# One transfer instead of seven for three chunks of w_down, in a decode step of attention and GEGLU FFN

## The chip, the cores and the metric

The kernel runs on one core of a Trainium2 chip. The metric is the device time of one execution in microseconds, as a median of runs. Beside it stands the profile of one execution, with the span from its first to its last instruction.

## The reference, cut to what matters

Two sequences (B = 2) each have one new token of D = 640 features. 32 heads of 192 attend to the last 2,048 of 8,192 cached positions; then follows a GEGLU FFN of width F = 1,536. All tensors are bfloat16.

```python
W = min(4096, max(256, Sk // 4))            # 2048 of Sk = 8192
q = (ln(x) @ wq).reshape(B, 1, 32, 192).transpose(0, 2, 1, 3)
k, v = k_cache[:, :, Sk - W:], v_cache[:, :, Sk - W:]
p = softmax(einsum("bhqd,bhkd->bhqk", q, k) * 192 ** -0.5)
o = einsum("bhqk,bhkd->bhqd", p, v)
h = x + o.transpose(0, 2, 1, 3).reshape(B, 1, 6144) @ wo
out = h + (gelu(ln(h) @ w_gate) * (ln(h) @ w_up)) @ w_down
```

Here `ln` is a layernorm without weights. Nearly all bytes are K and V, 50 MB each inside the window; the weights come to 21.6 MB.

## The kernel before, in words

**Memory.** All large inputs pass through one ring in SBUF, `ring` (L174): 128 partitions of 122,880 bytes. `load` (L251) gives each load the next place in the ring and puts it in a list. `pump` (L258) takes loads from this list in order and records one DMA for each on SP's queue (L272), as soon as the readers of the place's old content have been recorded; the DMA then waits on the chip until those readers are done. `done` (L275) marks a load as read and calls `pump`. So all transfers run in one order, on one queue: K of 16 groups of heads and V of the same groups alternating (3 MB each), with Wq near the start and Wo in between, and at the end Wo, w_gate, w_up and w_down. A group is four heads of one sequence.

**Parts.** A load may be cut along the partitions: `parts` is a list of ranges of partitions, and L271 to L273 issue one DMA for each range, with a completion semaphore of its own from a set of 32. A matmul that reads such a load waits for all of its parts. Only w_down uses this: `load_ffn` (L302) loads w_down (F x D, 1.97 MB) in four chunks of three of the twelve row blocks (`WDC`, L147), 480 KB each, with 3,840 bytes in each partition. For chunks 0 to 2 (`WDB = 3`, L149) the list `WDP` (L150) applies: partitions 0 to 111 in one DMA, then five DMAs of three partitions, then one of a single partition. Chunk 3 goes as one DMA of 128 partitions. In all these are 22 DMAs.

**Compute.** For each group, `transposes` turns K on TensorE through PSUM, ScalarE and VectorE copy it to SBUF, `scores`, `softmax` and `e_columns` give the weights, and `pv` (L571) multiplies V. After every four groups `o_rows` and `o_columns` arrange the result, and `oproj` (L616) multiplies it with Wo. `wo_parts` (L299) says in how many parts Wo of eight heads is loaded and multiplied: one of 12 rows per partition, or, for the last eight heads, two of 8 and 4.

**The end.** After the last `oproj`, `h_columns` (L643) and a layernorm give the FFN's input. `ffn_in` (L691) multiplies it with w_gate (20 matmuls, L697), `ffn_columns` (L703) turns the result by a copy on VectorE (L704) and three transposes (L708), and `h_rows` (L714) puts the residual into PSUM. A chain of small steps on VectorE and ScalarE then computes gelu of the gate. The second `ffn_in` takes w_up, `ffn_columns` again, and a product gives `uT`. Last, L737 to L747 multiply `uT` with w_down chunk by chunk, 12 matmuls each (L743), add to the residual in PSUM, and a copy (L749) and two small stores (L751) write the output. The order of the work on each engine is that in which the program records it.

Of the kernel before, what the change touches and what calls it, by code (L numbers as in the profile page):

```python
# [13 lines left out]
D = 640  # L14
# [28 lines left out]
class _Prog:  # L43
# [10 lines left out]

    def op(self, eng, fn, R=(), W=(), X=(), dma=None):
        o = _Op(eng, fn)
        deps = []

        def add(y, same_ok):
            if y is None or y is o:  # L60
                return
            if y.dma_sem is None and y.eng == eng and dma is None and same_ok:
                return
            deps.append(y)

        for t in R:
            add(self.w.get(t), eng == "pe")
        for t in W:
            add(self.w.get(t), eng == "pe")
            for y in self.r.get(t, ()):  # L70
                add(y, True)
        for t in X:
            for e, y in self.x.get(t, {}).items():
                if e != eng:
                    add(y, True)
        for t in R:
            self.r.setdefault(t, []).append(o)
        for t in W:
            self.w[t] = o
            self.r[t] = []  # L80
        for t in X:
            self.x.setdefault(t, {})[eng] = o
        if dma is not None:
            o.dma_sem = dma
            self.dma_count[dma] = self.dma_count.get(dma, 0) + 16
            o.dma_val = self.dma_count[dma]
        o.deps = deps
        lst = self.per.setdefault(eng, [])
        o.idx = len(lst) + 1
        lst.append(o)  # L90
        self.ops.append(o)
        return o
# [51 lines left out]
NSEM = 32  # L144
# [1 line left out]
WQC = ((0, 2), (2, 4), (4, 5))  # L146
WDC = ((0, 3), (3, 6), (6, 9), (9, 12))  # L147
BIG = 1.0e9
WDB = 3  # L149
WDP = ((0, 112), (112, 115), (115, 118), (118, 121), (121, 124), (124, 127), (127, 128))  # L150


def bass_sequential_preLN__sliding_block_cached__geglu_ffn__decode_kernel(
# [12 lines left out]
    with ExitStack() as ctx:  # L166
# [78 lines left out]
        P = _Prog()  # L245


        pos = [0, 0]
        where, live, queue, used = {}, [], [], set()

        def load(key, nbytes, src, shape, parts=((0, 128),)):  # L251
            if pos[0] + nbytes > RING:
                pos[0] = 0
            off, i = pos[0], pos[1]
            pos[0], pos[1] = off + nbytes, i + len(parts)
            queue.append((key, off, nbytes, src, shape, i, parts))

        def pump():  # L258
            while queue:
                key, off, nbytes, src, shape, i, parts = queue[0]  # L260
                old = [q for q in live if q[1] < off + nbytes and off < q[1] + q[2]]
                if any(q[0] not in used for q in old):
                    return
                for q in old:
                    live.remove(q)
                queue.pop(0)
                live.append((key, off, nbytes))
                v = shape(ring[:, off // 2:(off + nbytes) // 2])
                toks = [("ring", x) for x in range(off // GRAN, (off + nbytes + GRAN - 1) // GRAN)]
                where[key] = (v, toks + [("part", key, n) for n in range(1, len(parts))])  # L270
                for n, (p0, p1) in enumerate(parts):  # L271
                    P.op("sp", lambda e, v=v[p0:p1], src=src[p0:p1] if n or len(parts) > 1 else src: e.dma_start(v, src),  # L272
                         W=(toks if n == 0 else [("part", key, n)]) + [("sem", (i + n) % NSEM)], dma=f"d{(i + n) % NSEM}")  # L273

        def done(*keys):  # L275
            used.update(keys)
            pump()
# [5 lines left out]
        def load_k(g):  # L283
            load(("k", g), 2 * TPG * DH, kv_src(A_k_cache, g), lambda v: v)

        def load_v(g):
            load(("v", g), 2 * TPG * DH, kv_src(A_v_cache, g), lambda v: v)

        def load_wq():
            wq = A_wq.rearrange("(p c) n -> p c n", c=NC5)  # L290
            for i, (c0, c1) in enumerate(WQC):
                load(("wq", i), 2 * (c1 - c0) * HQ * DH, wq[:, c0:c1, :], lambda v: v.rearrange("p (c n) -> p c n", n=HQ * DH))
# [9 lines left out]
        def load_ffn():  # L302
            for key, w in (("wg", B_w_gate), ("wu", B_w_up)):
                load(key, 2 * NC5 * F, w.rearrange("(p c) f -> p c f", c=NC5),
                     lambda v: v.rearrange("p (c f) -> p c f", c=NC5))
            wd = B_w_down.rearrange("(r p j) n -> r p j n", p=128, j=3)
            for i, (f0, f1) in enumerate(WDC):
                load(("wd", i), 2 * (f1 - f0) * D, wd[i],
                     lambda v: v.rearrange("p (s n) -> p s n", n=D), WDP if i < WDB else ((0, 128),))


        def dve(fn, R=(), W=(), X=()):
            return P.op("dve", fn, R, W, X)

        def act(fn, R=(), W=(), X=()):
            return P.op("act", fn, R, W, X)
# [26 lines left out]
        load_wo(2)  # L343
        load_wo(3)
        load_ffn()
        pump()

        BITS = (1, 2, 3, 6, 12, 16, 28, 31, 32, 64, 96)
# [463 lines left out]
```

## Time and profile before

| What | Value |
|---|---|
| Median of 3 runs | 299.38 us (299.14 to 299.56) |
| Profiled execution, its own time | 299.38 us |
| Span of the profiled execution | 297.5 us |
| Mean granted TensorE clock | 0.83 |
| Busy: PE, PEld, DVE, ACT, POOL | 66%, 51%, 44%, 32%, 1% of the span |
| DMA, whole span | 122.61 MB, mean 412 GB/s |
| K and V transfers | 16 each, 3,072 KB; issue to landing 31.6 and 28.3 us (medians) |
| w_gate and w_up | 1,920 KB each; issue to landing 32.8 and 27.6 us |
| w_down issues | 3 of 420 KB, 1 of 480 KB, 15 of 11.2 KB, 3 of 3.8 KB |

PE is TensorE's matmuls and PEld its weight loads; DVE is VectorE, ACT ScalarE, POOL GpSimd, and SPq the queue of SyncE, which issues the DMAs. A line number stands for a line of the kernel. The 16 DMA engines of the core are given as one mean share. The trace also has a record of each DMA packet (start, duration, bytes; here one row of one partition), without its engine, and of each time that a DMA engine reports its part of a transfer done, which is called a landing record below.

### The profile page before, as it was taken

Reading aid. Unit: us, or ns where it says so; the run is one execution under the profiler, and the core shown is the slowest. Engines: PE = TensorE matmul, PEld = TensorE weight load, DVE = VectorE, ACT = ScalarE, POOL = GpSimd, SP = SyncE. Lnnn points to the kernel's source line nnn. Section 1 sums busy time; section 2 is a strip of 40 time slices with the busy share of each in tenths; the row PEclk is TensorE's granted clock in tenths of the full one; section 3 lists DMA queues with packets and bytes.
Section 4 is the critical chain, followed back from the end, with each engine's and each line's share of the span. In section 5 each row is a group of like instructions: output and inputs, shape, how many; then the busy total and the mean of one; then the engine's idle time right before and its main releaser. Section 6 shows DMA issues by size and latency. Waiting matters only on the chain.

```text
span 297.5 us, 4923 instructions
## 1 busy us (share of the span) xinstructions
PE 197.7 (66%) x2141; PEld 152.1 (51%) x2141; DVE 130.6 (44%) x326; ACT 95.5 (32%) x119; POOL 2.7 (1%) x19
## 2 busy tenths in 40 slices
PE   2473668749497497759591888774878674957554
PEld 1451266719294475456560858471748471934311
DVE  5950455716247154425263353461473461533121
ACT  2150134715233163325251324452324361420000
POOL 3000000000000000000000000000000000000000
PEclk9997559998869599959796695999797998697655
DMA  7999999999999999999999999999999999999993
GB/s 285 443 434 419 423 426 438 430 432 433 419 422 433 443 426 423 433 416 433 435 433 430 419 436 422 433 428 433 430 425 433 432 430 422 430 426 413 425 232 111
DMA packets 6713, 122.61 MB, mean 412 GB/s; under 512 B 802, under 2 KB 804, under 8 KB 1444
## 3 DMA queue, kind: packets, MB, share of 16 engines
q1 hardware_dynamic: 6680, 122.29, 97.7%
q8 instruction: 17, 0.28, 0.4%
q14 instruction: 4, 0.03, 0.0%
q10 hardware_dynamic: 12, 0.00, 0.0%
HBM read 122.29 MB, written 0.00 MB: 411 GB/s over the span
## 4 chain that ended last, share of the span: by engine, by line
DMA 69%; PE 20%; SPq 5%; DVE 3%; issue 1%; ACT 0%
DMA ring<-in_A_k_cache_dram 53%; PE tps L479 17%; DMA ring<-in_A_wq_dram 9%; DMA ring<-in_B_w_down_dram 6%; SPq L272 5%; PE ops L577 1%; DVE rq L331 1%; DVE ktr L491 1%; PE tps L501 1%; DVE ering L331 0%; PE m L628 0%; PE m L610 0%; PE ops L519 0%; ACT qrow L508 0%; PE m L591 0%
## 5 line engine op out<-in xcount | busy, mean ns | idle before, releaser
L479 PE MATMUL tps<-identf,ring 128*128 128x128 f32 x768 | 116.2, 320 | 45.9 <-DMA ring<-in_A_k_cache_dram 45.0
L479 PEld LDWEIGHTS tps<-identf,ring 128*128 128x128 f32 x768 | 107.5, 169 | 49.2 <-DMA ring<-in_A_k_cache_dram 46.2
L488 ACT ACTIVATE ktr<-tps 128x1024 bf16<-128x1024 bf16 x80 | 79.2, 1023 | 87.1 <-PE tps L479 86.6
L491 DVE COPY ktr<-tps 128x1024 bf16<-128x1024 bf16 x112 | 74.4, 688 | 73.8 <-PE tps L479 73.1
L552 ACT ACTIVATE eexp<-sm,nm 128x512 bf16<-128x512 f32 x16 | 11.5, 721 | 66.8 <-DVE nm L550 66.8
L577 PE MATMUL ops<-ring,ering 128*32 128x384 bf16 x512 | 24.9, 338 | 5.6 <-DMA ring<-in_A_v_cache_dram 5.5
L541 DVE CUSTOM_DVE_ANT_1 sm<-sps,mska 128x512 f32<-128x512 f32 x16 | 11.1, 691 | 36.2 <-PE sps L535 36.2
L535 PE MATMUL sps<-ktr,rq 128*16 128x512 bf16 x384 | 26.0, 405 | 0.3 <-DVE rq L331 0.3
L577 PEld LDWEIGHTS ops<-ring,ering 128*32 128x32 bf16 x512 | 12.7, 99 | 14.2 <-DMA ring<-in_A_v_cache_dram 6.8
L535 PEld LDWEIGHTS sps<-ktr,rq 128*16 128x16 bf16 x384 | 9.5, 90 | 11.5 <-issue 2.8
L548 PEld LDWEIGHTS m<-mrhs,pm 128*128 128x128 bf16 x16 | 1.5, 96 | 25.0 <-DVE mrhs L327 25.0
L548 PE MATMUL m<-mrhs,pm 128*128 128x16 bf16 x16 | 2.9, 184 | 16.9 <-DVE mrhs L327 16.9
L501 PE MATMUL tps<-ring,xnT 128*32 128x384 bf16 x80 | 5.7, 444 | 7.3 <-DMA ring<-in_A_wq_dram 7.3
L331 DVE TENSOR_TENSOR rq<-ops,mask 128x96 bf16<-128x96 f32 x16 | 2.7, 248 | 14.3 <-PE ops L519 14.3
L331 DVE TENSOR_TENSOR ering<-m,mask 128x256 bf16<-128x256 f32 x16 | 6.7, 420 | 2.4 <-PE m L561 2.4
L501 PEld LDWEIGHTS tps<-ring,xnT 128*32 128x32 bf16 x80 | 2.3, 119 | 10.2 <-DMA ring<-in_A_wq_dram 8.4
L383 ACT ACTIVATE lt<-m,eps_t 128x2 f32<-128x2 f32 x2 | 0.5, 262 | 19.4 <-PE m L381 19.4
L561 PE MATMUL m<-sel,eexp 128*128 128x64 bf16 x64 | 4.8, 201 | 1.2 <-ACT eexp L552 1.2
L628 PE MATMUL m<-ring,ot 128*2 128x320 bf16 x96 | 4.1, 298 | 1.9 <-DMA ring<-in_A_wo_dram 1.9
L331 DVE TENSOR_TENSOR orow<-m,wm 128x1536 bf16<-128x1536 f32 x3 | 5.3, 1751 | 0.0
L561 PEld LDWEIGHTS m<-sel,eexp 128*128 128x128 bf16 x64 | 4.4, 105 | 1.6 <-DVE nm L550 1.3
L610 PE MATMUL m<-selb,orow 128*128 128x2 bf16 x48 | 3.5, 200 | 2.2 <-DVE ering L331 1.6
(112 smaller groups left out, 79.6 us busy)
## 6 DMA issues: line engine op xcount, KB each, us to landing
ring<-in_A_k_cache_dram SPq DMA_DIRECT2D x16, 3072.0 KB, 31.6
ring<-in_A_v_cache_dram SPq DMA_DIRECT2D x16, 3072.0 KB, 28.3
ring<-in_A_wq_dram SPq DMA_DIRECT2D x2, 3072.0 KB, 20.9
ring<-in_A_wo_dram SPq DMA_DIRECT2D x3, 1920.0 KB, 27.7
ring<-in_B_w_gate_dram SPq DMA_DIRECT2D x1, 1920.0 KB, 32.8
ring<-in_B_w_up_dram SPq DMA_DIRECT2D x1, 1920.0 KB, 27.6
ring<-in_A_wq_dram SPq DMA_DIRECT2D x1, 1536.0 KB, 27.8
ring<-in_A_wo_dram SPq DMA_DIRECT2D x1, 1280.0 KB, 28.0
```

What stands on the lines that cost most here:

```text
L272: P.op("sp", lambda e, v=v[p0:p1], src=src[p0:p1] if n or len(parts) > 1 else src: e.dma_start(v, src), W=(toks if n == 0 else [("part", k ...
L331: return lambda e: e.tensor_tensor(out=out, in0=a, in1=b, op=op)
L479: ins = e.transpose(tps[bi][:, 128 * u:128 * (u + 1)], kv[:, off:off + 128], identf[:, :])
L488: act(lambda e, dst=dst, bv=bv: e.activation(out=dst, in_=bv, func=ACT.Copy), W=[("kt", slot, n)], X=[("t", bi)])
L491: dve(lambda e, dst=dst, bv=bv: e.tensor_copy(dst, bv), W=[("kt", slot, n)], X=[("t", bi)])
L501: ins = e.matmul(tps[0][32 * r:32 * (r + 1), 0:384], lhsT=xnT[:, c, 32 * J:32 * (J + 1)], rhs=wq[:, c - c0, 1536 * J + 384 * r:1536 * J + ...
L535: ins = e.matmul(sps[32 * ch:32 * ch + 16, :], lhsT=rq[:, g, k, :], rhs=ktr[:, g % 2, k // 2, 1024 * ch + k % 2:1024 * (ch + 1):2], start= ...
L541: dve(lambda e: e.tensor_tensor_reduce(out=sm[:, :].rearrange("p (u x) -> p u x", u=4), in0=sps[:, :].rearrange("p (u x) -> p u x", u=4), ...
L548: pe(lambda e: e.matmul(m2[:, 256:272], lhsT=pm[:, :], rhs=mrhs[:, :], start=True, stop=True), R=["pm", "mrhs"], X=["m2"])
L552: act(lambda e: e.activation(out=eexp[:, :], in_=sm[:, :], func=ACT.Exp, bias=nm[:, 0:1], scale=1.0, accum_out=zr[:, g // 4 % 2, g % 4:g % ...
L561: ins = e.matmul(o, lhsT=eexp[:, 128 * u:128 * (u + 1)], rhs=sel64[:, :], start=True, stop=True)
L577: ins = e.matmul(ops_[32 * r:32 * (r + 1), 0:384], lhsT=ering[:, g % 4, t, :], rhs=vv[:, 384 * t:384 * (t + 1)], start=(g % 4 == 0 and t < 4),
```

## The change

The list of parts is taken out of `load` and `pump`, and with it `WDB` and `WDP`. Each load is one DMA of 128 partitions and has one semaphore. So w_down is loaded with four DMAs of 480 KB instead of 22. The places in the ring, the order of the loads and the matmuls stay; only the numbers of the semaphores shift. Wo of the last eight heads is loaded and multiplied in two parts of 8 and 4 rows per partition in both kernels.

```diff
-WDB = 3
-WDP = ((0, 112), (112, 115), (115, 118), (118, 121), (121, 124), (124, 127), (127, 128))
...
-        def load(key, nbytes, src, shape, parts=((0, 128),)):
+        def load(key, nbytes, src, shape):
...
-            pos[0], pos[1] = off + nbytes, i + len(parts)
-            queue.append((key, off, nbytes, src, shape, i, parts))
+            pos[0], pos[1] = off + nbytes, i + 1
+            queue.append((key, off, nbytes, src, shape, i))
...
-                where[key] = (v, toks + [("part", key, n) for n in range(1, len(parts))])
-                for n, (p0, p1) in enumerate(parts):
-                    P.op("sp", lambda e, v=v[p0:p1], src=src[p0:p1] if n or len(parts) > 1 else src: e.dma_start(v, src),
-                         W=(toks if n == 0 else [("part", key, n)]) + [("sem", (i + n) % NSEM)], dma=f"d{(i + n) % NSEM}")
+                where[key] = (v, toks)
+                P.op("sp", lambda e, v=v, src=src: e.dma_start(v, src), W=toks + [("sem", i % NSEM)],
+                     dma=f"d{i % NSEM}")
...
-                     lambda v: v.rearrange("p (s n) -> p s n", n=D), WDP if i < WDB else ((0, 128),))
+                     lambda v: v.rearrange("p (s n) -> p s n", n=D))
```

More of the change, by code (lines that the diff above doesn't have):

```diff
@@ L254, in load @@
             off, i = pos[0], pos[1]
-            pos[0], pos[1] = off + nbytes, i + len(parts)
-            queue.append((key, off, nbytes, src, shape, i, parts))
+            pos[0], pos[1] = off + nbytes, i + 1
+            queue.append((key, off, nbytes, src, shape, i))
         def pump():
             while queue:
-                key, off, nbytes, src, shape, i, parts = queue[0]
+                key, off, nbytes, src, shape, i = queue[0]
                 old = [q for q in live if q[1] < off + nbytes and off < q[1] + q[2]]
```

## The prediction

> **What bounds the kernel now.** I first read the page's busy slices, then its chain of waits, then the end of the chain in order of time, then tables of short windows over the last 20 us. The page says that the DMA engines carry the run, and that something happens in its last two slices:
>
> ```profile
> DMA  7999999999999999999999999999999999999993
> GB/s 285 443 434 419 423 426 438 430 432 433 419 422 433 443 426 423 433 416 433 435 433 430 419 436 422 433 428 433 430 425 433 432 430 422 430 426 413 425 232 111
> ...
> DMA 69%; PE 20%; SPq 5%; DVE 3%; issue 1%; ACT 0%
> ```
>
> The reader should see that the last slice but one (282.6 to 290.1 us) is as busy as all others, at 9 tenths, but moves 232 GB/s instead of about 425. The engines are not idle there; they are slow. The chain ends on a w_down transfer, one group of matmuls and the output:
>
> ```profile
> 275.53 18.62 DMA ring<-in_B_w_down_dram
> 294.15 0.04 issue
> 294.19 0.60 PE m L743 x10
> ```
>
> The 5% of SPq ahead of this in the chain is the 22 w_down issues, one after another. It is not a cause. The last issue, at 275.53, joined a queue that had 11 us or more of earlier packets before it; its first packets ran near 288. The table by windows of 2 us (stretch, length, busy time of PE, PEld, DVE, ACT, POOL, then granted clock, DMA share, GB/s) shows when the loss begins:
>
> ```profile
> 280.00:282.00 2.00, 0.59 (x2) 0.50 (x2) 0.63 (x5) 0.47 (x2) 0.00 (x0) 0.50 0.99 415
> 282.00:284.00 2.00, 1.77 (x20) 0.52 (x20) 0.13 (x2) 0.00 (x0) 0.00 (x0) 0.50 1.03 311
> 284.00:286.00 2.00, 1.41 (x11) 0.57 (x11) 1.04 (x5) 0.00 (x0) 0.00 (x0) 0.50 1.02 238
> 286.00:288.00 2.00, 0.00 (x0) 0.00 (x0) 0.83 (x4) 0.22 (x1) 0.00 (x0) 0.50 1.00 230
> 288.00:290.00 2.00, 1.48 (x20) 0.51 (x20) 0.00 (x0) 0.00 (x0) 0.00 (x0) 0.50 0.97 204
> ```
>
> The packet records (start, duration, bytes) give the moment: the first packet of 3,840 bytes, a w_down row, starts at 282.27. Until then a w_up or w_gate row of 15,360 bytes takes 573 to 587 ns. From then on such rows, of the very same w_up transfer, take 629, 704, 855 and then 909 to 1,039 ns, on all nine engines that still work on w_up. w_down rows start at 149 ns and take 230 to 340 ns between 283 and 290.4. Those nine are behind: the landing records of w_gate show seven engines done at 278.16 to 279.11 and nine at 281.06 to 281.48; of w_up, seven at 282.77 to 284.09 and nine at 287.49 to 288.48.
>
> [...] 16 landings for a 112-row part, 3 for a 3-row part, 1 for the single row. [...] Inside the 112-row parts the durations swing between 149-160 ns and 200-250 ns in steps of a few rows, for all active engines together (291.4 fast, 291.75 slow, 292.0 medium, 292.3 slow), and from 292.8, when only the last chunk (128 partitions) is left, nearly all rows take 149 ns, with 12 engines at work. That chunk has the same row size and comes from the same tensor.
>
> **The change, part by part.** Wo: both kernels load and multiply Wo of the last heads in two parts of 8 and 4 rows; no line of that changes. Cost 0. What changes is w_down chunks 0 to 2: each goes from seven DMAs to one of 128 partitions.
>
> Issues on SP: 18 fewer, of 0.24 to 1.83 us each. The four that stay take some 0.4 us each after 261.28; the fourth waits for PE's work on group 14 (ends 262.29), so all are out near 263, not 276.6. Gain at the end 0: the queue is served in order and full until 282.27. If this cover were gone, no issue would start the data sooner than 282.27 either. Nothing else waits behind them on SP but the output store at 295.
>
> PE waits: 18 fewer semaphore checks. In the timeline 24 weight loads over two chunks took 0.63 us, 12 of the last chunk 0.23; the 14 waits of the first two cost at most 0.17 us, and they lie ahead of a wait for data. Value 0, bounds 0 and -0.2.
>
> w_down rows: [...] For the nine late engines that is 3 x 149 = 0.45 us more work at the undisturbed duration.
>
> The slowdown: here I choose full speed, as for every 128-partition transfer in this trace, the Wo parts (5,120-byte rows at 196 to 206 ns) among them. Bounds of this term: no slowdown left, or all of it left (the rivals).
>
> Sum for the nine late engines. w_gate lands at 281.48 on the last of them. w_up: 8 rows x 577 ns = 4.62 us, so 286.10 (check: the first engine went from 278.16 to 282.77, 4.61 us, mostly undisturbed). w_down: 4 chunks x (8 x 149 ns + some 20 ns for the completion) = 4 x 1.21 = 4.84 us, so the last chunk lands at 290.94, against 294.15 now.
>
> Does PE keep up? Now the second FFN product starts 0.04 after w_up lands, at 288.52:
>
> ```profile
> 288.52 1.77 PE L697 MATMUL ops<-ring,hnT 128*2 128x384 bf16 x20 [2.59 <-DMA ring<-in_B_w_up_dram]
> ...
> 292.06 1.63 PE L743 MATMUL m<-ring,uT 128*2 128x160 bf16 x36 [0.34 <-DVE uT L331]
> 294.19 0.57 PE L743 MATMUL m<-ring,uT 128*2 128x160 bf16 x12 [0.50 <-DMA ring<-in_B_w_down_dram]
> 294.81 0.33 DVE L749 CAST yrow<-m 98x160 bf16<-98x160 f32 x1 [2.81 <-PE m L743]
> ```
>
> With w_up at 286.10 it starts at 286.14 (h_rows before it ends at 285.93, so PE is free). The copy after it on DVE needs the gate's chain done: that ends at 287.18, before 287.95. From its start to the first down product is 292.06 - 288.52 = 3.54 us, so down starts at 289.68. Three chunks issue in about 0.63 + 0.26 = 0.9 us, to 290.6. The fourth is then the wait that ends last: 290.94 + 0.04 = 290.98 in place of 294.19. All after it is as now, so the gain is 3.21 us. The profiled execution took 299.38 with a span of 297.5; it equals the median of the runs. 299.38 - 3.21 = **296.2 us**, span 294.3.
>
> This has a floor: if w_down came at once, PE would start the fourth chunk at 290.6, 0.4 us earlier; if w_up did too, h_rows' end saves 0.17 more. Hence 295.6.
>
> **Rivals.**
> (a) Partly: slow in part for another reason, such as rows of only 3,840 bytes from a tensor being read beside w_up. At 200 ns a row instead of 149, 32 rows take 6.4 us: landing 286.10 + 6.4 = 292.5, gain 1.65, time 297.7. For it: the 112-row parts showed 174 to 220 ns in between. Against: Wo's 5,120-byte rows, beside other transfers, were undisturbed, and the last chunk ran at 149.
> (b) Slower: the slowdown comes from reading w_down at all, in whatever parts, while more than 12 engines are active. For it: the rate rose when four engines had finished near 290.4. Then w_up stays slow, and the late engines have three more rows of some 270 ns, 0.81 us, on the tail: 294.15 becomes 294.96, time 300.2. It decides from a mean row of about 201 ns if w_up stays slow too: from w_up's last packets near 287.2 to the end of the last row at 293.66 there is room for 32 rows of 201 ns. Against: 12 engines ran chunk 1 at 149 to 160 ns for a while (290.6 to 290.9), and with it, slower again, until 292.7; a limit by the number of engines would not swing.
> (c) No difference: half-way between (a) and (b), rows at about 230 ns with w_up undisturbed: 286.10 + 32 x 0.23 = 293.5, landing near 294; time 299.3.
>
> **How the numbers follow.** Forecast 68%, own range 295.5 to 297.0; its lower end is the floor, its upper end rows of some 175 ns, as in the better stretches of the 112-row parts (286.10 + 32 x 0.175 = 291.7, time 297.0); the runs shown spread over 0.42 us. (a) 13%, 297.0 to 298.8; (c) 5%, 298.8 to 300.0; (b) 14%, above 300.0. The range goes from the floor less a tenth, 295.5, to 298.9, the far end of (a), and leaves out some 2 in 10. A measurement of this kernel can tell about 0.2% (0.6 us) from no change: faster 81%, same 5%, slower 14%.
>
> **What would show it.** Right: in the windows from 282 to 286 the rate stays above 400 GB/s; no w_up row exceeds some 600 ns; w_up's wait ends near 286.1; w_down rows take about 150 ns, and the last lands near 291. Wrong: rows of 230 ns or more and 240 GB/s from 282.3 on, though every transfer has 128 partitions; then the split was a relief for the late engines, not the cause.

## The result, and the profile after

The changed kernel takes 296.08 us (median of 6 runs, 295.85 to 296.27), the kernel before 299.43 in the same comparison (299.06 to 299.62). The ratio is 0.9889, with a 95% interval from 0.9877 to 0.9902: 3.35 us less. The profiled execution has a span of 294.3 us, against 297.5. The forecast was 296.2, with a span of 294.3.

First the page's line of transfer rates in 40 slices, which answers to the one of before:

```profile
DMA  7999999999999999999999999999999999999992
GB/s 268 431 429 445 449 428 426 428 426 424 426 418 433 423 438 431 428 424 438 433 416 446 430 424 423 428 428 430 428 426 431 430 438 423 428 431 411 429 407 113
```

The slice that moved 232 GB/s at full business now moves 407. The table by windows of the changed kernel (stretch, length, busy time of PE, PEld, DVE, ACT, POOL, granted clock, DMA share, GB/s) has the same stretches as the one of before:

```profile
280.00:282.00 2.00, 0.78 (x3) 0.60 (x3) 0.66 (x4) 0.26 (x1) 0.00 (x0) 0.50 1.01 422
282.00:284.00 2.00, 1.51 (x20) 0.51 (x20) 0.17 (x1) 0.20 (x1) 0.00 (x0) 0.50 0.98 407
284.00:286.00 2.00, 1.34 (x15) 0.57 (x11) 0.80 (x3) 0.00 (x0) 0.00 (x0) 0.50 0.94 386
286.00:288.00 2.00, 2.00 (x28) 0.52 (x20) 1.14 (x6) 0.22 (x1) 0.00 (x0) 0.50 0.87 348
288.00:290.00 2.00, 0.99 (x15) 0.65 (x15) 0.74 (x2) 0.00 (x0) 0.00 (x0) 0.50 0.57 232
```

Two things are to be seen. From 282 to 288 the rate is some 100 to 150 GB/s higher than before. From 288 to 290 it falls to 232 GB/s together with the DMA share (0.57): here engines are done, whereas before they were busy (0.97) and slow, at 204 GB/s. The packet records say it more sharply:

```
after the first w_down packet       before     after
w_up rows (15,360 B), median ns        941       578
w_up rows, longest                   1,039       586
w_down rows (3,840 B), median ns       242       149
w_down rows, longest                   519       162
w_up landed, us                     288.48    286.23
last of w_down landed, us           294.15    290.91
```

The end of the chain in order of time (start, length, what) no longer has a w_down transfer in it:

```profile
285.68 0.64 PE m L715 x8
286.33 1.74 PE ops L696 x20
288.07 0.02 issue
288.09 0.57 DVE grow L703
...
289.57 0.19 DVE uT L330
289.76 0.04 issue
289.81 1.80 PE m L742 x44
```

On the timeline the lines that answer to those of before are these (start, length, engine, instruction, count, idle time before it and what ended it):

```profile
285.61 0.71 PE L715 MATMUL m<-hrow,hsel 98*2 98x160 f32 x8
...
286.27 0.10 PEld L696 LDWEIGHTS ops<-ring,hnT 128*2 128x2 bf16 x8 [0.55 <-DMA ring<-in_B_w_up_dram]
286.27 1.77 PE L696 MATMUL ops<-ring,hnT 128*2 128x384 bf16 x20
...
289.81 1.77 PE L742 MATMUL m<-ring,uT 128*2 128x160 bf16 x48 [0.34 <-DVE uT L330]
...
291.63 0.33 DVE L748 CAST yrow<-m 98x160 bf16<-98x160 f32 x1 [1.88 <-PE m L742]
```

The second FFN product starts at 286.27 in place of 288.52, and the 48 matmuls with w_down run in one piece, with no wait for data that the timeline shows. The second FFN product (L696) starts as w_up lands: its first weight load was waiting for w_up, and starts 0.04 us after the landing at 286.23. The chain puts the residual (L715) ahead of it, because by the profile that ends at 286.32. The two lie within 0.1 us, so it is not shown how much an earlier w_up would still gain.

### The profile page after: what moved, and what is told of

Its sections match the earlier page's. It is cut to its first block, busy times and chain, and to the rows that moved or that the text cites. A ratio compares the mean times of both kernels' runs of the same rounds, so it can differ in the third digit from the quotient of the medians.

```text
span 294.3 us, 4896 instructions
## 1 busy us (share of the span) xinstructions
PE 198.8 (68%) x2141; PEld 152.4 (52%) x2141; DVE 130.4 (44%) x326; ACT 95.6 (32%) x119; POOL 2.7 (1%) x19
## 4 chain that ended last, share of the span: by engine, by line
DMA 69%; PE 24%; DVE 4%; SPq 1%; issue 1%; ACT 0%; DVEq 0%; ACTq 0%
DMA ring<-in_A_k_cache_dram 50%; PE tps L478 17%; DMA ring<-in_A_wo_dram 10%; DMA ring<-in_A_wq_dram 10%; PE ops L576 1%; DVE rq L330 1%; PE m L627 1%; SPq L271 1%; PE sps L696 1%; PE m L742 1%; PE m L609 1%; PE ops L696 1%; PE tps L707 1%; PE tps L500 1%; PE m L646 0%
## 5 line engine op out<-in xcount | busy, mean ns | idle before, releaser
L478 PE MATMUL tps<-identf,ring 128*128 128x128 f32 x768 | 115.0, 318 | 48.4 <-DMA ring<-in_A_k_cache_dram 47.3
L627 PE MATMUL m<-ring,ot 128*2 128x320 bf16 x96 | 5.7, 379 | 0.3 <-DVE ot L613 0.3
L586 DVE COPY osb<-ops 128x192 f32<-128x192 f32 x8 | 2.5, 354 | 5.8 <-PE ops L576 5.8
```

Source lines behind the costliest of these rows:

```text
L478: ins = e.transpose(tps[bi][:, 128 * u:128 * (u + 1)], kv[:, off:off + 128], identf[:, :])
L627: ins = e.matmul(m1[32 * r:32 * r + 2, 192:512], lhsT=ot[:, J % 2, kk, :], rhs=wo[:, kk - k0, 320 * h:320 * (h + 1)], start=(kk == 1 or J ...
```

## The experiments

All times are medians; in the three comparisons the kernel before had 299.41, 299.24 and 299.31 us. What had to be told apart: which property of the seven parts made the transfers slow (the place of the rows in SBUF, the addresses in HBM, the size of the parts or their number), and then how far the harm reaches. Theory P puts the loss down to the partitions in SBUF that the rows go to, theory A to the addresses in HBM, theory S to the small parts, theory N to the number of DMAs. The packet records don't name the engine, so no view here shows which engine writes which partition. The runs show at which partitions added rows did harm (e3, e6 and e10 to e12) and at which they did none (e5 and e9); why it is these partitions is not shown.

### e1: partitions 0 to 111, and 112 to 127

```diff
-WDP = ((0, 112), (112, 115), (115, 118), (118, 121), (121, 124), (124, 127), (127, 128))
+WDP = ((0, 112), (112, 128))
```

> Chunks 0 to 2 of w_down go as one DMA of partitions 0 to 111 and one of 112 to 127, six DMAs in place of 21. Theory P [...]: the 112-row parts alone bring the slowdown back; w_up rows above 800 ns from about 282.3 us on, 298.5 to 300 us. Theory S (the parts of three rows and one row[...]): they are gone, so near the changed kernel, 296.0 to 296.8. Theory N (the number of DMAs, 18 more of them to issue, to report and to wait for): 3 more instead of 18, so a sixth of the difference, 296.4 to 296.8.

Measured: 299.47 us, ratio to before 1.000 (0.9991 to 1.0009). The whole loss is there with 3 more DMAs than in the changed kernel instead of 18. w_up rows have a median of 958 ns after w_down has begun, w_down rows 246. The parts of three rows are not needed for the loss, and the number of DMAs does not explain it. Theory P had this.

### e2: partitions 0 to 111 alone

```diff
+WDP = ((0, 112),)
```

> Only partitions 0 to 111 of w_down chunks 0 to 2 are loaded; the last 16 rows of each are left out, so 184 KB fewer bytes and no more DMAs than in the changed kernel. Theory P: still slow, 240 to 280 GB/s from 282 to 286 us, 297.5 to 299 us although it moves less. Theories S and N: faster than the changed kernel by up to 0.45 us (three rows of 149 ns fewer on every engine), 295.6 to 296.1, and rows of 149 ns throughout.

Measured: 298.93 us, ratio 0.9984 (0.9976 to 0.9992). With as many DMAs as the changed kernel and 184 KB fewer bytes it is 2.85 us slower than it. The windows of this kernel show the busy, slow engines of before:

```profile
282.00:284.00 2.00, 1.66 (x20) 0.52 (x20) 0.17 (x1) 0.08 (x1) 0.00 (x0) 0.50 1.03 305
284.00:286.00 2.00, 1.34 (x15) 0.57 (x11) 0.92 (x3) 0.00 (x0) 0.00 (x0) 0.50 1.02 248
286.00:288.00 2.00, 0.17 (x4) 0.00 (x0) 1.02 (x5) 0.22 (x1) 0.00 (x0) 0.50 0.96 213
```

A DMA share of 0.96 to 1.03 beside 213 to 305 GB/s is the mark to look for. So it is the 112-row transfer itself. Against e1 the 16 rows of each chunk that are left out are worth 0.54 us.

### e3: whole chunks, and the small parts once more

```diff
 P.op("sp", ... e.dma_start(v, src) ...)
+if key[0] == "wd" and key[1] < 3:
+    for p0, p1 in EXTRA:          # (112, 115) ... (124, 127), (127, 128)
+        P.op("sp", ... e.dma_start(ktr[p0:p1, 0, key[1], 0:1920], src[p0:p1]) ...)
```

> The changed kernel with one DMA of 128 partitions for each chunk, and behind each of chunks 0 to 2 the six small DMAs (five of three rows, one of one row) once more, into a part of SBUF that nobody reads[...]. Theory P: [...] 296.0 to 297.0. Theory S: as before the change, 298.5 to 299.5. Theory N: 18 more DMAs, as before the change, 298.5 to 299.5.

Measured: 297.91 us, ratio 0.9946 (0.9931 to 0.9961), 1.83 us slower than the changed kernel. No theory had this: theory P had too little, the two others too much. Half of the w_up rows (23 of 47) exceed 650 ns, the longest takes 1,033. A part of three rows has three landing records in the trace of before, and one of a single row has one; so parts that run on three engines or one, with 48 rows in all, suffice to slow the others for a while. Small parts and their number are still one thing here; e9 takes them apart.

### e4: 64 and 64 partitions

```diff
+WDP = ((0, 64), (64, 128))
```

> Chunks 0 to 2 as two DMAs of 64 partitions[...]. Theory P: w_down rows near 298 ns (twice 149) while such a part runs, w_up rows slowed too, 298.5 to 301 us. Theory A [...]: undisturbed, 296.0 to 296.6. Theory N: 3 more DMAs, 296.4 to 296.8.

Measured: 300.13 us, ratio 1.0022 (1.0015 to 1.0028): slower even than before. Theory A fails here as it was put, with 296.0 to 296.6; how the rows of such a part are dealt out to the engines is not shown, and e9 to e11 do without this. Two halves of the partitions, which look like a harmless cut, cost 4.05 us for 1.47 MB. w_up rows have a median of 943 ns, w_down rows one of 241 ns, less than the 298 of theory P.

### e5 and e6: DMAs of one row, into partitions 0 to 2 and into 124 to 126

A part of one row has a single landing record in the trace of before, so one engine carries it. Both kernels add 18 such DMAs with the same source rows; only the partition differs.

```diff
+    p = 0 + key[1]        # e5; in e6: 124 + key[1]
+    for place in range(6):
+        P.op("sp", ... e.dma_start(<row p of ktr, place>, src[key[1]:key[1] + 1]) ...)
```

> The changed kernel, with six DMAs of one row each behind each of w_down chunks 0 to 2, 18 in all. [...] these rows go to partitions 0 to 2[...], into a part of SBUF that nobody reads. Theory P [...]: nobody is disturbed[...]: 296.0 to 296.5, w_up rows at most 600 ns. Theory N (many DMAs as such): about 297.9, as with the 18 small parts of the earlier run.

> As the run before it, but the 18 rows, from the same source rows, go to partitions 124 to 126[...]. Theory P: [...] w_up rows of at least one engine exceed 800 ns[...]: 296.8 to 298.0. Theory N: the same time as the run before it, within 0.3 us.

Measured: e5 296.05 us, ratio 0.9893 (0.9878 to 0.9908), as the changed kernel; e6 296.83, ratio 0.9919 (0.9903 to 0.9936). So 18 more small DMAs cost nothing at partitions 0 to 2, and at 124 to 126 they cost 0.78 us more. Same bytes, same source, same queue, same number: what is left is the place in SBUF. In e5 one of the seven early engines lands its share of the last chunk 2.7 us later than its like, at 290.44, as 18 rows of 149 ns (2.68 us) would have it, and still ahead of the nine late ones. So, by its times, one engine carried all 18 rows; it is an early one and has this time to spare.

The packet records of e6 add what I had not expected. Only 26 of the w_down rows exceed 170 ns, nearly always two at a time, most of them (18) with 284 to 314 ns (twice 149 is 298). The longest w_up row has 595 ns against 586 in the changed kernel, where theory P expected more than 800. So the slow rows came in pairs, each taking about twice as long as otherwise, and the other rows were hardly touched. I had taken one such pair for enough to slow all; that was an assumption of mine.

Nor do the 0.78 us come from the others. Fifteen engines have the last chunk landed by 290.86, as in e5 (290.87); one lands at 291.63. By its times this is the engine with the added rows: the last of these lands at 290.71, and its share of the last chunk comes 0.92 us behind it (in e5 0.90 us behind).

### e7 and e8: the same cut in the middle of the run

w_down is whole; Wo of the second eight heads (15,360 bytes in each partition) is cut instead.

```diff
-load(("wo", J, i), ..., src[:, k0:k1, :], ...)
+load(("wo", J, i), ..., src[:, k0:k1, :], ..., WOP if J == 1 else ((0, 128),))
+WOP = ((0, 112), (112, 128))        # e7; in e8: ((0, 64), (64, 128))
```

> w_down whole as in the changed kernel; instead Wo of the second eight heads (15,360 bytes in each partition, half-way through the run, 1.97 MB) goes as partitions 0 to 111 and 112 to 127. Theory P: its rows take 800 to 1,150 ns in place of 577, its 1.97 MB move at some 250 GB/s in place of 425, and as the DMA engines never idle, all of the 3.2 us is in the time: 298.5 to 300.0. A theory by which only the tail of the run is sensitive, or only rows of 3,840 bytes: 296.0 to 296.5.

> As the run before it, with Wo of the second eight heads as two DMAs of 64 partitions. Theory P: [...] rows of up to 1,154 ns (twice 577), 213 to 260 GB/s for 1.97 MB, 3 to 4.6 us: 299.0 to 300.7, and slower than with 112 and 16. Addresses in HBM, or only the tail: 296.0 to 296.5.

Measured: e7 302.59 us, ratio 1.0112 (1.0097 to 1.0127); e8 302.48, ratio 1.0108 (1.0093 to 1.0124). Both are 6.4 to 6.5 us slower than the changed kernel, twice what I had expected of e7, and they don't differ, though theory P had e8 slower. Windows of 4 us, first of the changed kernel, then of e7:

```profile
150.00:154.00 4.00, 3.48 (x36) 3.13 (x38) 3.15 (x10) 2.05 (x2) 0.00 (x0) 0.97 0.97 412
154.00:158.00 4.00, 3.77 (x62) 1.99 (x61) 2.15 (x7) 1.02 (x1) 0.00 (x0) 1.00 1.03 441
158.00:162.00 4.00, 0.12 (x1) 0.03 (x1) 1.62 (x2) 0.81 (x2) 0.00 (x0) 0.81 1.03 442
```

```profile
150.00:154.00 4.00, 3.09 (x30) 2.86 (x34) 3.03 (x9) 2.31 (x3) 0.00 (x0) 1.00 0.99 224
154.00:158.00 4.00, 3.77 (x61) 2.02 (x61) 1.68 (x6) 0.24 (x1) 0.00 (x0) 1.00 0.97 207
158.00:162.00 4.00, 0.11 (x1) 0.02 (x1) 1.61 (x2) 0.81 (x2) 0.00 (x0) 1.00 1.13 225
```

The rate is halved from the moment the first engine begins the cut transfer (149.6 us) until the last one ends it (162.5). That is 12.9 us, of which about half, some 6 us, is lost. I had counted only the 1.97 MB of the transfer itself, at 250 GB/s, but the windows have 207 to 225, and 2.9 MB move in this stretch. The engines don't begin and end the transfer together, and while any of them is in it, all are slow: rows of K and V that overlap this stretch have a median of 1,745 ns and up to 2,660, where they otherwise take 916. And since the DMA engines have hardly any idle time before the end (in the changed kernel a busy share of 90% or more in every slice but the first and the last), nearly all of it is in the time.

### e9 to e12: how many rows in a DMA, and at which partitions

Behind each of chunks 0 to 2 come four DMAs of three rows (e12: two rows); only the partitions differ.

```diff
+    p = (0, 1)[n // 6]        # e9: rows p, p+4, p+8      low partitions, four apart
+    p = (64, 65)[n // 6]      # e10: rows p, p+4, p+8     middle partitions, four apart
+    p = (124, 92)[n // 6]     # e11: rows p, p+1, p+2     three neighbours, high partitions
+    p = (124, 92)[n // 6]     # e12: rows p, p+1          two neighbours, high partitions
```

> The changed kernel with four DMAs of three rows behind each of w_down chunks 0 to 2 (12 in all[...], into a part of SBUF that nobody reads), at partitions 0, 4, 8 or 1, 5, 9[...]. Theory P [...]: nobody disturbed, 296.0 to 296.4, w_up rows below 600 ns. Theory N (small DMAs on three engines as such): 297.0 to 298.0, w_up rows above 800 ns as in the run with the small parts added.

> As the run before it, at partitions 64, 68, 72 or 65, 69, 73[...]. Theory L [...]: w_up rows either below 600 or near 1,150 ns, on at most three engines[...], 296.1 to 298.0. Theory B [...]: most w_up rows between 700 and 1,000 ns, 297.0 to 298.5.

> As before, at partitions 124 to 126 or 92 to 94[...]. Theory L: all engines suffer, w_up rows of 700 to 1,100 ns on all late engines, 297.3 to 298.5. Theory B: the same or less than with three pairs[...].

> As before with parts of two rows[...] at partitions 124, 125 or 92, 93[...]. [...] w_up rows above 650 ns on all late engines, 296.8 to 298. If not: rows of 3,840 bytes near 450 ns on three engines, w_up rows below 600 ns, 296.3 to 297.2.

Measured, with the runs above for comparison (added rows by their partitions; w_up rows after the first w_down packet, about 46 to 52 rows in each record):

```
                                    time us   ratio to before          w_up rows ns:   longest w_down
                                                                      median  longest    row ns
changed kernel                       296.08   0.9889 (0.9877-0.9902)     578      586      162
e5  1 row at 0, 1 or 2               296.05   0.9893 (0.9878-0.9908)     578      581      162
e9  3 rows at 0,4,8 or 1,5,9         296.15   0.9896 (0.9882-0.9911)     576      581      162
e6  1 row at 124, 125 or 126         296.83   0.9919 (0.9903-0.9936)     578      595      314
e12 2 rows at 124,125 or 92,93       296.92   0.9923 (0.9909-0.9938)     585      629      407
e3  3 rows or 1, in 112 to 127       297.91   0.9946 (0.9931-0.9961)     640    1,033      384
e10 3 rows at 64,68,72 or 65,69,73   298.45   0.9972 (0.9961-0.9983)     596      973      319
e11 3 rows from 124 or from 92       298.62   0.9978 (0.9970-0.9986)     584    1,194      627
```

e9 settles e3: small DMAs of three rows cost nothing at partitions 0, 4, 8 and 1, 5, 9 (296.15 us against 296.08). The source rows of e9, e10 and e11 are the same, so the addresses in HBM are not the cause either. Theories L and B are about who suffers: by L, in e10, only the engines whose rows delay each other, at most three; by B all of them, and more so the more engines are delayed. Both were ideas of mine and no view shows either at work. e10 ends theory L: 19 of 50 w_up rows exceed 650 ns. Nine of them start between 283.63 and 283.96 us and take 809 to 973 ns, so they overlap; if an engine takes one row after the other, as 4.63 us for eight rows of 578 ns in the changed kernel have it, they lie on nine engines.

Theory B fits better, but not well: it had most w_up rows of e10 between 700 and 1,000 ns, and their median is 596. Two rows at neighbouring partitions, of which e12 asks whether they are enough to slow all, hardly harm the others. What the runs show is an order: with DMAs of one row at 124 to 126 the w_up rows take at most 595 ns, with two rows at neighbouring partitions up to 629 (9% more than 578), and with three, in e3, e10 and e11, they take up to twice as long for part of the time.

Not all of this time was lost by the others. In order, the thirteenth of the sixteen landings of the last w_down chunk, which leaves out the latest three, comes at 290.76 us in the changed kernel, 290.77 in e9, 290.81 in e6, 290.87 in e12, 292.03 in e10, 292.38 in e11 and 292.68 in e3. So e6 and e12 lose hardly more than the time of the few engines that come last, in e10 and e11 some 1.0 us of the 2.4 and 2.5 lost belongs to these few, and in e3 all is shared.

The window from 284 to 286 us of e10 and of e11, where 386 was moved by the changed kernel:

```profile
284.00:286.00 2.00, 1.34 (x15) 0.57 (x11) 0.92 (x3) 0.00 (x0) 0.00 (x0) 0.50 0.84 269
```

```profile
284.00:286.00 2.00, 1.34 (x15) 0.56 (x11) 0.86 (x3) 0.00 (x0) 0.00 (x0) 0.50 0.97 229
```

How three added rows at a time hold up the rows of other transfers is not settled. No run here looks at it.

## Why the prediction was right

**The slowdown is the parts' and goes with them.** Right. The choice of full speed for this term was the step that decided, and the w_up rows after (at most 586 ns) and the w_down rows (median 149) show it. e1, e2 and e4 bring the loss back by the cut alone. For the added rows the place in SBUF is shown as the cause: e9 against e10 and e11 slows all engines by nothing else. That the same holds for the 112-row parts is concluded from this and is not shown: no view shows which engine writes which of their rows, and the cut may move the rows of an engine in HBM as well as in SBUF.

**One pair of rows that delay each other slows all.** This was my assumption, and it is wrong. In e6 such pairs take 284 to 314 ns a row, and the w_up rows at most 3% longer (595 against 578 ns). Among the added DMAs only those of three rows had a heavy effect (e3, e10, e11), and those not at every partition (e9). The sum was not touched by this, since it needs only that all slowdown goes with the parts.

**The late engines' sum.** w_gate landed at 281.60, not 281.48; w_up at 286.23, against 286.10 (4.63 us for eight rows against 4.62); the last w_down chunk at 290.91 against 290.94. So the four chunks took 4.68 us, not 4.84. The landings of one chunk after the other lie 1.16 to 1.20 us apart, about eight rows of 149 ns (1.19), so the 20 ns per chunk that I had put in for the completion were too much.

**What is late next.** Here one step failed, without harm. I had the fourth chunk's data as the wait that ends last. The three chunks before it do not issue in 0.9 us: the records of the single matmuls have a group of four every 0.133 us, and the fourth chunk starts at 290.96, 1.15 us after the first. Its data landed at 290.91. So both were ready at the same time, and the chain goes through PE instead. The down products ended at 291.58; my sum gave 290.98 + 0.57 = 291.55. The term for 36 matmuls was too small by 0.25 us, and the first of them started 0.13 us later than in the sum. Together they used up the 0.4 us by which the sum had PE ahead of the data; that they did no more is luck. The floor of 295.6 was too low for the same reason: at this pace PE would not have been ready for the fourth chunk any earlier, had w_down come at once.

**SP's issues at nothing.** Right, though not all were out near 263: the fourth took 3.54 us and ended at 265.87. The queue was full until the first w_down row at 282.36, so this cost nothing. SPq fell from 5% of the chain to 1%, with DMA at 69% in both, as the page's chain says:

```profile
DMA 69%; PE 24%; DVE 4%; SPq 1%; issue 1%; ACT 0%; DVEq 0%; ACTq 0%
```

That the time followed from this fall is disproved by e5. There 18 DMAs are issued again, and the time is that of the changed kernel. For the 18 waits that PE has fewer e5 says nothing, as nobody reads its rows; e2 does, which has no such wait more than the changed kernel and still loses 2.85 us.

**The relief for the late engines.** The 0.45 us for three rows at 149 ns are an estimate of mine: a part of 112 rows has 16 landing records, as a whole chunk has, which makes seven rows for each engine in place of eight, if they are shared out evenly. Against the 3.3 us that the cut cost it does not show. e1, with the last 16 rows in one DMA in place of six, takes as long as before (299.47 us, ratio 1.000): there the relief and what the small parts cost on top are not told apart, and together they come to nothing.

**The rivals.** (a), rows of some 200 ns from small rows or from w_up beside them, fails with the median of 149 ns while w_up ran beside them. (b), reading w_down at all, and (c), rows of about 230 ns, fail likewise: with all 16 engines active, no w_down row took more than 162 ns. The measure named for "right", over 400 GB/s in every window from 282 to 286, was a little too strict: the second of them has 386.

## What to carry to other kernels

Look for stretches in which the DMA share is near 1 and the rate is low: in this kernel rows of the same bytes took longer in such stretches (w_up rows 941 ns in place of 578 at the median, at 230 to 311 GB/s), and bytes were not the limit. A load that is cut along the partitions, in 112 and 16 or even in two halves, was slow itself here, and all transfers beside it were slow as long as any engine was in it: 3.3 us lost at the tail with 112 partitions, 6.5 us in the middle. To give less work to late engines by moving partitions to other engines, try where the rows may go in SBUF, and don't only count who carries them: the same 18 rows cost nothing at partitions 0 to 2 and 0.78 us at 124 to 126. A cut along the free dimension, as in the two Wo parts of 8 and 4 rows, kept the full rate (5,120-byte rows at a median of 198 ns).

## What the runs showed of the hardware that was not expected

- The harm to other rows grew steeply with the number of rows in an added DMA. With one at partitions 124 to 126, most of the w_down rows that were slow took 284 to 314 ns in place of 149, and the w_up rows at most 3% more; with two at neighbouring partitions (124, 125 and 92, 93) the w_up rows took up to 9% more (629 against 578 ns); with three, up to twice as long (1,194 against 578 ns).
- Three rows four partitions apart, at 64, 68, 72 and 65, 69, 73, cost nearly as much as three neighbours from 124 or 92 (298.45 and 298.62 us), and at 0, 4, 8 and 1, 5, 9 nothing (296.15 us against 296.08).
- Halves of 64 partitions were at least as bad as 112 and 16: 302.48 and 302.59 us for Wo, 300.13 and 299.47 for w_down.
- In the changed kernel, where every load is one DMA of 128 partitions, a row's time went with its bytes: 149, 198, 388, 576 and 914 ns (medians) for 3,840, 5,120, 10,240, 15,360 and 24,576 bytes.
- Nine of the 16 engines were 2.2 to 3.4 us behind the other seven at w_up's landing, in the changed kernel as in e5. Where this comes from was not tried.
